# Turning part of the token tiles with VectorE blocks and transfers through DRAM instead of on TensorE, in a delta-rule attention followed by an MLP mixer

## The chip, the cores and the metric

One core of a Trainium2 chip runs the kernel. The metric is the device time of one execution in microseconds (us). Engines are named as the profile names them: PE is TensorE (PEld its weight loads), DVE is VectorE, ACT is ScalarE, POOL is GpSimd and SP is SyncE, whose queue (SPq) issues all transfers of this kernel.

## The reference

Four batch elements, eight heads, 768 tokens, head size 48. A delta-rule recurrence runs over the tokens; its output, seen as 768 tokens x 384 features, goes through a token-mixing and a channel-mixing MLP, each with a residual.

```python
k_n = k / (norm(k) + 1e-6);  state = 0                      # per element and head
for t in range(768):
    y[t]  = q[t] @ state
    state = state + beta[t] * outer(k_n[t], v[t] - k_n[t] @ state)

x  = y as (4, 768, 384)
u  = x + (relu(x.T @ w_tok1) @ w_tok2).T                    # token mixing, 768 -> 256 -> 768
out = u + relu(u @ w_ch1) @ w_ch2                           # channel mixing, 384 -> 1536 -> 384
```

All of it is fp32.

## The kernel before

**Order.** The kernel is a set of generators, one per piece of work, and a string written out by hand says which of them takes its next step. An engine executes its instructions in the order in which they were traced; the waits between engines follow from the data and from the buffers. So the string fixes the order on every engine and on SP's queue. The names in it: `k`, `v` load rows of a pair of chunks, `p` prepares them, `c` and `d` form their products, `t` sends triangular blocks to DRAM (`n_dram`), `i` inverts a round of them on DVE and writes the result (`w_dram`), `f` fetches it (`gm<-w_dram`), `j` joins it, `r` is one step of the recurrence, and `m0` to `m3` are the mixers of the four elements. A mixer begins when its element's recurrence is done, and runs beside the recurrence of the next one. Element 3's mixer runs at the end, beside the last steps of element 2's; what comes after has nothing beside it.

**The mixer.** `mixer(b)` works on `xb`, 128 tokens x 6 tiles x 384 features. First the token phase: `p_1` (L1009), ACT's Relu, and for each of the six tiles c `p_h` (L1022), which DVE adds into `xb[:, c]` (L1026). Then the tokens go in three pairs of tiles (c = 0, 2, 4). For each pair `turn_pair(c)` makes `u_t`, the pair with features on the partitions: for each tile three PE transposes into the PSUM tile `p_ut` (L1032) and one ACT copy (L1036). For elements 1 to 3 (`b >= FAST`) it goes on with `forms(u_t)`, eleven DVE sums of 128x128 blocks (L950), six steps of the generator, some into `t_c` and `t_d`, some in place in `u_t`. `wide_fast` multiplies these forms with sums of the weights in 15 products (L981, PSUM tile `p_r`), which ACT and DVE gather into `r2` (L990, L993, L997). While it ends, DVE makes `s1` and `s2` from `r2` (L1063). Seven products (L1111) in the order a11, a12, s2, s1, a21, a12, a22, twelve (in the middle: six and six) matmuls each, accumulate alternately in `p_o` and `p_o2`, and DVE adds each into `xb` (L1040). Between a11's and the first a12's product stands `turn_pair` of the next pair. `store` writes a finished tile out (L1043).

**Buffers.** `u_t` has one buffer. `t_d`, `s1` and `s2` share the tag `d64` with three buffers, with the staging tiles of the weights early on. The mixer's PSUM tiles (`p_1`, `p_h`, `p_ut`, `p_r`, `p_o`, `p_o2`) share three banks; a tile takes its bank when it is first written.

The order string lets the mixers of elements 2 and 3 overlap so: element 3's six `p_h` steps come while element 2's last pair has done a11, and its `s2` and `s1` products come after them.

Of the kernel before, what the change touches and what calls it, by code (L numbers as in the profile page):

```python
# [8 lines left out]
FP32 = mybir.dt.float32  # L9
# [5 lines left out]
U = 128  # L15
DP = 64
HB = 32
# [6 lines left out]
def kernel(  # L24
# [39 lines left out]
    nc = tc.nc  # L64
# [3 lines left out]
    DM = H * D  # L68
# [15 lines left out]
    loads = ctx.enter_context(tc.tile_pool(name="loads", bufs=2))  # L84
# [6 lines left out]
    dram = ctx.enter_context(  # L91
        tc.tile_pool(name="dram", bufs=2, space=bass.MemoryType.DRAM)
    )
# [7 lines left out]
    def ps_mlp(shape, name):  # L101
        return psum.tile(shape, FP32, name=name, tag="mlp", bufs=3)
# [19 lines left out]
    for i in range(2):  # L122
        r = slice(C * i, C * i + C)
# [25 lines left out]
    for kept, shape in ((kpad, [H, DP]), (qpad, [H, DP]), (kst_of, [NP, 2, D])):  # L149
        for _ in range(NL, NK):  # L150
            n = H * shape[-1]
            flat = lent[:, at : at + n]
# [45 lines left out]
    FAST = 1  # L198
# [7 lines left out]
    for a in cuts[:2]:  # L206
        g = a + NB * GW
# [52 lines left out]
    def piece_of(w, j, col):  # L260
        assert (id(w), j, col - col % WP) in rounded
        return w[:, j]
# [275 lines left out]
    def z_of(u):  # L538
# [9 lines left out]
        out=low16,  # L548
        in_=ident.rearrange("s (q t) -> s q t", t=HB)[:, :, QB:HB],
# [5 lines left out]
        out=even,  # L555
        in_=ident.rearrange("s (q t) -> s q t", t=C)[:, :, 0:HB],
# [4 lines left out]
        out=odd, in0=even, scalar1=-1.0, scalar2=1.0, op0=ALU.mult, op1=ALU.add  # L561
    )
    sides = const.tile([128, 2], FP32, name="sides")
    for i, side in enumerate((even, odd)):
        nc.vector.tensor_tensor(
            out=sides[:, i : i + 1], in0=low16, in1=side, op=ALU.mult
# [435 lines left out]
    def mixer(b):  # L1002

        xb = xbs[b]
        p_1 = [ps_mlp([128, DM], "p_1") for _ in range(NDH)]
        for c in range(NCH):
            assert written.issuperset([NQ * b + 2 * c, NQ * b + 2 * c + 1])
            for dh in range(NDH):
                nc.tensor.matmul(  # L1009
                    p_1[dh], piece_of(w1, c, 0)[:, dh * 128 : (dh + 1) * 128], xb[:, c],  # L1010
                    start=(c == 0), stop=(c == NCH - 1),
                )
            yield
        r1 = []
        for dh in range(NDH):
            r = mlp_pool.tile([128, DM], FP32, name="r1")
            nc.scalar.activation(r, p_1[dh], ACTF.Relu)
            r1.append(r)
        for c in range(NCH):
            p_h = ps_mlp([128, DM], "p_h")  # L1020
            for j in range(NDH):
                nc.tensor.matmul(  # L1022
                    p_h, piece_of(w2, j, c * 128)[:, c * 128 : (c + 1) * 128], r1[j],
                    start=(j == 0), stop=(j == NDH - 1),
                )
            nc.vector.tensor_tensor(out=xb[:, c], in0=xb[:, c], in1=p_h, op=ALU.add)  # L1026
            yield

        def turn(u_t, c):
            p_ut = ps_mlp([128, NCB, 128], "p_ut")  # L1030
            for cb in range(NCB):
                nc.tensor.transpose(  # L1032
                    p_ut[:, cb], xb[:, c, cb * 128 : (cb + 1) * 128], ident
                )
            i = c % 2 * U
            nc.scalar.copy(u_t[:, :, i : i + U], p_ut)  # L1036

        def add(c, half, p):
            e = slice(DH * half, DH * half + DH)
            nc.vector.tensor_tensor(out=xb[:, c, e], in0=xb[:, c, e], in1=p, op=ALU.add)  # L1040

        def store(c, e=slice(0, DM)):
            nc.sync.dma_start(out=out[b, c * 128 : (c + 1) * 128, e], in_=xb[:, c, e])  # L1043

        def turn_pair(c):
            u_t = mlp_pool.tile([128, NCB, 2 * U], FP32, name="u_t", bufs=1)
            for i in range(2):
                turn(u_t, c + i)
                yield
            if b < FAST:  # L1050
                return u_t, None
            f = yield from forms(u_t)
            return u_t, f

        u_t, t_c = yield from turn_pair(0)
        for c in range(0, NCH, 2):

            r2 = mlp_pool.tile([128, NM, 2, 2 * U], FP32, name="r2", bufs=1)
            a11, a12 = r2[:, :, 0, 0:U], r2[:, :, 1, 0:U]
            a21, a22 = r2[:, :, 0, U : 2 * U], r2[:, :, 1, U : 2 * U]  # L1060

            def combine(out, x, y, op, ms):
                nc.vector.tensor_tensor(out=out[:, ms], in0=x[:, ms], in1=y[:, ms], op=op)  # L1063

            made = []

            def halves_of(ms):
                if not made:
                    made.extend(
                        loads.tile([128, NM, U], FP32, name=n, tag="d64", bufs=3)  # L1070
                        for n in ("s1", "s2")
                    )
                s1, s2 = made
                combine(s1, a21, a22, ALU.add, ms)
                combine(s2, s1, a11, ALU.subtract, ms)
                combine(a21, a11, a21, ALU.subtract, ms)

            if b >= FAST:
                for ms in wide_fast(t_c, r2):
                    if ms is not None:  # L1080
                        halves_of(ms)
                    yield
            else:
                for m in range(NM):
                    p_c = ps_mlp([128, 2, 2 * U], "p_c")
                    for k in range(2):
                        f = 2 * m + k
                        for cb in range(NCB):
                            nc.tensor.matmul(  # L1089
                                p_c[:, k],  # L1090
                                piece_of(wc1, cb, f * 128)[:, f * 128 : (f + 1) * 128],
                                u_t[:, cb], start=(cb == 0), stop=(cb == NCB - 1),
                            )
                        if (b, c) == (FAST - 1, NCH - 2):
                            used.add(f)
                        if k == 0:
                            yield
                    nc.scalar.activation(r2[:, m], p_c, ACTF.Relu)
                    yield
                    if m % (NM // 2) == NM // 2 - 1:  # L1100
                        halves_of(slice(m + 1 - NM // 2, m + 1))
                        yield

            s1, s2 = made
            turns = (*range(2, NM), 0, 1) if b >= FAST else range(NM)

            def product(p, a, j, start):
                for i, m in enumerate(turns):
                    block = (2 * m + j // 2,) if j in (0, 2, 3) else (m, "sum", j)
                    assert (id(wc2), *block) in rounded  # L1110
                    nc.tensor.matmul(  # L1111
                        p, a[:, m], wc2[:, m, j],
                        start=(start and i == 0), stop=(i == NM - 1),
                        skip_group_check=True,
                    )
                    if i == NM // 2 - 1:
                        yield


            p_o = ps_mlp([128, DH], "p_o")  # L1120
            p_o2 = ps_mlp([128, DH], "p_o2")
            yield from product(p_o, a11, 0, True)
            add(c, 0, p_o)
            yield
            if c + 2 < NCH:
                u_t, t_c = yield from turn_pair(c + 2)
            yield from product(p_o2, a12, 2, True)
            add(c, 0, p_o2)
            yield
            for ms in (slice(0, NM // 2), slice(NM // 2, NM)):  # L1130
                combine(a12, a12, s2, ALU.subtract, ms)
            yield from product(p_o, s2, 5, False)
            add(c, 1, p_o)
            yield
            yield from product(p_o2, s1, 4, True)
            add(c + 1, 1, p_o2)
            yield
            yield from product(p_o, a21, 1, False)
            add(c + 1, 1, p_o)
            final = (b, c) == (B - 1, NCH - 2)  # L1140
            if final:
                store(c + 1, slice(DH, DM))
            yield
            yield from product(p_o2, a12, 3, False)
            add(c, 1, p_o2)
            store(c)
            yield
            yield from product(p_o, a22, 6, False)
            add(c + 1, 0, p_o)
            store(c + 1, slice(0, DH) if final else slice(0, DM))  # L1150
            yield
# [17 lines left out]
    for b in range(B):  # L1169
        jobs[f"m{b}"] = mixer(b)  # L1170
# [112 lines left out]
    for word in order.split():  # L1283
        name, _, n = word.partition("*")
# [34 lines left out]
```

## Time and profile before

| | us |
|---|---|
| median of the runs | 639.97 (639.02 to 641.68, 3 runs) |
| span of the profiled execution, first to last instruction | 635.6 |
| PE busy in that span | 611.4 |
| DVE busy | 442.5 |
| ACT busy | 261.0 |
| SP queue's transfers, share of 16 DMA engines | 34.7% |

The profiled execution's own device time was not kept beside its span; the median of the runs lies 4.4 us above the span. The mean granted TensorE clock of the span is 0.995. In the profile's lines a group reads: line, engine, operation, output<-input, shapes, count, then busy time and mean ns of one, then the idle time of the engine ahead of it and who ended it. In the chain and the timelines the first two numbers are the start (us from the span's start) and the duration.

### The profile page before, as it was taken

The numbers are of one execution on the slowest core, as the hardware profiler recorded it, in microseconds if no ns is written. First come the engines' busy times: TensorE is split into PE (matmuls) and PEld (weight loads), VectorE is DVE, ScalarE is ACT, GpSimd is POOL, SyncE is SP. The second block draws the span as 40 slices with busy tenths as digits, with TensorE's granted clock in tenths as the row PEclk, the third lists the DMA queues.
The fourth block names the chain that finished last, engine by engine and source line by source line (L and its number), as shares of the span: only waits on it lengthen the run. The fifth ranks groups of instructions, "written<-read, shape, count | busy, mean of one in ns | idle before, by whom it ended". The sixth has DMA issues, their size and how long they took to land.

```text
span 635.6 us, 21584 instructions
## 1 busy us (share of the span) xinstructions
PE 611.4 (96%) x9168; PEld 530.8 (84%) x9168; DVE 442.5 (70%) x1132; ACT 261.0 (41%) x631; POOL 108.2 (17%) x147
## 2 busy tenths in 40 slices
PE   7498899999999999999999999999999999999997
PEld 5457787577888988859899999779999977999997
DVE  4985877997879657987969997785627253373643
ACT  7759887436412243025615333044334130223240
POOL 2438363243210111011110020000000000000000
PEclk9889999999999999999999999999999999999999
DMA  9786667636542454243453213202010000000000
GB/s 172 183 159 149 155 150 188 159 90 146 103 119 64 85 111 110 66 114 74 99 106 87 51 63 69 47 14 36 13 40 3 26 2 1 26 1 25 2 26 26
DMA packets 135776, 50.27 MB, mean 79 GB/s; under 512 B 114656, under 2 KB 130144, under 8 KB 135680
## 3 DMA queue, kind: packets, MB, share of 16 engines
q1 hardware_dynamic: 135680, 48.89, 34.7%
q8 instruction: 72, 1.18, 0.8%
q14 instruction: 24, 0.20, 0.1%
HBM read 39.42 MB, written 9.44 MB: 77 GB/s over the span
## 4 chain that ended last, share of the span: by engine, by line
PE 77%; DVE 4%; ACT 3%; SPq 2%; DMA 1%; issue 1%; DVEq 0%; ACTq 0%
PE p_o L1111 24%; PE p_r L981 19%; PE p_c L1089 6%; PE p_h L1022 5%; PE p L1009 5%; PE p_k L813 3%; PE p_y L833 2%; PE p_s L851 2%; PE p_g L442 2%; PE p_z L773 2%; PE p_y L852 1%; PE p_ut L1032 1%; PE p_w L837 1%; PE p_warm L227 1%; DMA x<-n_dram 1%
## 5 line engine op out<-in xcount | busy, mean ns | idle before, releaser
L1111 PE MATMUL p_o<-wc,r 128*128 128x192 f32 x720 | 127.5, 330 | 0.7 <-ACT u_t L1036 0.6
L1111 PEld LDWEIGHTS p_o<-wc,r 128*128 128x128 f32 x720 | 116.5, 190 | 3.6 <-ACT u_t L1036 1.1
L993 DVE TENSOR_TENSOR r<-r,p_r 128x512 f32<-128x512 f32 x90 | 60.0, 685 | 48.3 <-PE p_r L981 47.7
L990 ACT COPY r<-p_r 128x512 f32<-128x512 f32 x54 | 31.4, 585 | 97.0 <-PE p_r L981 97.0
L1040 DVE TENSOR_TENSOR xb<-xb,p_o 128x192 f32<-128x192 f32 x84 | 29.3, 350 | 53.9 <-PE p_o L1111 53.7
L680 DVE TENSOR_TENSOR x<-x,sub 128x84 f32<-128x84 f32 (+24 forms) x178 | 58.2, 327 | 6.1
L676 DVE TENSOR_TENSOR sub<-x 128x84 f32<-128x84 f32 (+24 forms) x178 | 57.8, 325 | 6.5 <-DMA x<-n_dram 2.5
L1111 PE MATMUL p_o<-wc,s 128*128 128x192 f32 x288 | 50.5, 329 | 0.3 <-DVE xb L1040 0.3
L1089 PE MATMUL p_c<-u_t,wc 128*128 128x256 f32 x216 | 50.2, 384 | 0.1
L1111 PEld LDWEIGHTS p_o<-wc,s 128*128 128x128 f32 x288 | 46.8, 190 | 1.2 <-DVE xb L1040 0.6
L416 POOL TENSOR_TENSOR v_st<-v_st,nrm 128x384 f32<-128x384 f32 x24 | 20.3, 845 | 153.0 <-DMA v_st<-in_v_dram 121.6
L442 PE MATMUL p_g<-kq 48*64 48x128 f32 (+1 forms) x704 | 37.0, 282 | 8.9 <-ACT kq L511 6.6
L997 ACT ACTIVATE r<-r 128x512 f32<-128x512 f32 x54 | 33.9, 631 | 28.2 <-DVE r L993 27.9
L1089 PEld LDWEIGHTS p_c<-u_t,wc 128*128 128x128 f32 x216 | 39.9, 190 | 5.7 <-ACT u_t L1036 0.4
L865 ACT ACTIVATE xb<-p_y 64x192 f32<-64x192 f32 x96 | 31.1, 324 | 29.4 <-DMA out_dram<-xb 13.8
L499 POOL TENSOR_TENSOR mb<-mask_c,cs 128x512 f32<-128x512 f32 x20 | 20.9, 1045 | 129.8 <-DVE gm L445 85.8
L981 PE MATMUL p_r<-u_t,wc 128*128 128x128 f32 x288 | 38.9, 278 | 0.0
L442 PEld LDWEIGHTS p_g<-kq 48*64 48x64 f32 (+1 forms) x704 | 25.9, 136 | 14.6 <-ACT kq L511 9.3
L981 PE MATMUL p_r<-t_d,wc 128*128 128x128 f32 x288 | 37.7, 281 | 0.0
L981 PEld LDWEIGHTS p_r<-u_t,wc 128*128 128x128 f32 x288 | 35.3, 192 | 0.5
L981 PEld LDWEIGHTS p_r<-t_d,wc 128*128 128x128 f32 x288 | 34.1, 191 | 1.0
L843 ACT COPY w_t<-p_w 128x192 f32<-128x192 f32 x48 | 15.2, 316 | 46.2 <-PE p_w L837 45.0
(176 smaller groups left out, 1247.4 us busy)
## 6 DMA issues: line engine op xcount, KB each, us to landing
d<-in_moe_w_ch_dram SPq DMA_DIRECT2D x24, 384.0 KB, 4.5
v_st<-in_v_dram SPq DMA_DIRECT2D x96, 48.0 KB, 2.6
out_dram<-xb SPq DMA_DIRECT2D x23, 192.0 KB, 1.9
kst<-in_k_dram SPq DMA_DIRECT2D x64, 48.0 KB, 3.1
n_dram<-gm SPq DMA_DIRECT2D x72, 32.0 KB, 2.1
pads<-in_k_dram SPq DMA_DIRECT2D x24, 96.0 KB, 3.1
pads<-in_q_dram SPq DMA_DIRECT2D x24, 96.0 KB, 2.6
gm<-w_dram SPq DMA_DIRECT2D x72, 32.0 KB, 2.1
```

Of the source, the lines that this page charges most:

```text
L442: nc.tensor.matmul(p_g[PAR[i ^ cc], p], kqt[f, p, cc, 0], kqt[f, p, cc])
L676: nc.vector.tensor_tensor(out=tmp, in0=col.to_broadcast(dims), in1=row.to_broadcast(dims), op=ALU.mult,)
L680: nc.vector.tensor_tensor(out=new, in0=new, in1=tmp, op=ALU.add)
L865: nc.scalar.mul(y[:, :, D * i : D * i + D], p_y[PAR[1 - i]], 1.0 if c else -1.0)
L981: nc.tensor.matmul(p[:, i], pieces[i // width][:, at : at + 128], f[f"u{n}"], start=first and i == 0, stop=True, skip_group_check=True,)
L990: nc.scalar.copy(o, p)
L993: nc.vector.tensor_tensor(out=o, in0=o, in1=p, op=ALU.add if sign > 0 else ALU.subtract)
L997: nc.scalar.activation(o, o, ACTF.Relu)
L1009: nc.tensor.matmul(p_1[dh], piece_of(w1, c, 0)[:, dh * 128 : (dh + 1) * 128], xb[:, c], start=(c == 0), stop=(c == NCH - 1),)
L1022: nc.tensor.matmul(p_h, piece_of(w2, j, c * 128)[:, c * 128 : (c + 1) * 128], r1[j], start=(j == 0), stop=(j == NDH - 1),)
L1089: nc.tensor.matmul(p_c[:, k], piece_of(wc1, cb, f * 128)[:, f * 128 : (f + 1) * 128], u_t[:, cb], start=(cb == 0), stop=(cb == NCB - 1),)
L1111: nc.tensor.matmul(p, a[:, m], wc2[:, m, j], start=(start and i == 0), stop=(i == NM - 1), skip_group_check=True,)
```

## The change

For elements 1 to 3 and tiles 2 to 5, DVE transposes the tile in blocks of 32x32 as soon as the `p_h` sum is in it, into a staging tile `u_z` (tag `d64`, one for two tiles). Four transfers per tile write the blocks to a DRAM tile of 384 features x 256 tokens, so that a block's row becomes a run of 32 tokens (128 bytes) of one feature's row. `turn_pair` of these two pairs then issues a single transfer from DRAM into `u_t` in place of six PE transposes and two ACT copies. The eleven sums of `forms` no longer stand in `turn_pair` but are taken in steps behind the sums of the s2, s1, a21 and a12 products; `turn_pair` keeps its eight steps, so the order string stays as it is. The first pair of each element, and all of element 0, stay as they were.

```diff
     def mixer(b):
         xb = xbs[b]
+        away = {}
...
             nc.vector.tensor_tensor(out=xb[:, c], in0=xb[:, c], in1=p_h, op=ALU.add)
+            if b >= FAST and c >= 2:
+                if c % 2 == 0:
+                    flat = loads.tile([128, 2, DM], FP32, name="u_z", tag="d64", bufs=3)
+                    away[c] = dram.tile([DM, 2 * U], FP32, name="u_dram")
+                nc.vector.transpose(flat[:, c % 2], xb[:, c])
+                rows = away[c - c % 2].rearrange("(g j) t -> j g t", j=HB)
+                for t in range(U // HB):
+                    r = slice(HB * t, HB * t + HB)
+                    i = c % 2 * U + HB * t
+                    nc.sync.dma_start(
+                        out=rows[:, :, i : i + HB],
+                        in_=flat[r, c % 2].rearrange("p (g n) -> p g n", n=HB),
+                    )
             yield
...
+        coming = []
         def turn_pair(c):
             u_t = mlp_pool.tile([128, NCB, 2 * U], FP32, name="u_t", bufs=1)
+            if c in away:
+                nc.sync.dma_start(
+                    out=u_t, in_=away.pop(c).rearrange("(k f) t -> f k t", f=128)
+                )
+                coming.append(forms(u_t))
+                for _ in range(8):
+                    yield
+                return u_t, None
...
+        def form():
+            if coming:
+                try:
+                    next(coming[0])
+                except StopIteration as end:
+                    coming.clear()
+                    return end.value
...
             yield from product(p_o, s2, 5, False)
             add(c, 1, p_o)
             yield
+            form()
             yield from product(p_o2, s1, 4, True)
             add(c + 1, 1, p_o2)
+            form()
+            form()
             yield
             yield from product(p_o, a21, 1, False)
             add(c + 1, 1, p_o)
+            form()
+            form()
...
             yield from product(p_o2, a12, 3, False)
             add(c, 1, p_o2)
+            form()
+            t_c = form() or t_c
             store(c)
```

## The prediction

> **What bounds the kernel now.** I read the page's busy shares and chain first, then the chain in order of time, the group of the removed instruction, and the timelines of VectorE (DVE) and of SyncE's queue (SPq) in the three stages that change.
>
> ```profile
> span 635.6 us, 21584 instructions
> PE 611.4 (96%) x9168; PEld 530.8 (84%) x9168; DVE 442.5 (70%) x1132; ACT 261.0 (41%) x631; POOL 108.2 (17%) x147
> PE 77%; DVE 4%; ACT 3%; SPq 2%; DMA 1%; issue 1%; DVEq 0%; ACTq 0%
> L1032 PE MATMUL p_ut<-ident,xb x72: 272/273/329, 133.2 to 592.2; 128*128 128x128 f32 x72
> ...
> 319.54 0.81 PE p_ut L1032 x6
> 354.75 0.65 PE p_ut L1032 x6
> 449.65 0.65 PE p_ut L1032 x6
> 486.21 0.81 PE p_ut L1032 x6
> 563.13 0.34 PE p_ut L1032 x3
> 563.55 0.49 ACT u_t L1036
> 564.08 12.08 PE p_o L1111 x72
> 591.78 0.34 PE p_ut L1032 x3
> 592.73 12.07 PE p_o L1111 x72
> ```
>
> The first three lines are the page's: TensorE (PE) is busy 96% of the span and holds 77% of the chain that ended last. The fourth is the group of the transposes. The rest is the chain in order of time. There the second and third pairs of elements 1 to 3 show up, two tiles of three transposes each, and all of them lie on the chain: whatever PE saves there, the kernel saves, unless something else becomes late. The order of work is written out by hand and every engine takes its queue in order, so one late instruction holds all behind it.
>
> **What is removed.** 36 transposes, 12 ACT copies and, in element 3, a wait. Elements 1 and 2 save the four chain pieces: 0.81 + 0.65 + 0.65 + 0.81 = 2.92 us. In element 3 the product that follows a pair starts at 564.08, 0.95 after the transposes at 563.13: p_o2 gets its PSUM bank only when the first copy has emptied p_ut. The other pair is the same (592.73 - 591.78 = 0.95). Without p_ut the bank is free, so 1.90. Sum of the gain: **4.82 us**. ACT's copies save nothing more: it is busy 41% and the chain shows it only in these waits.
>
> The Trainium skill (TensorE: Matmul & The Clock Gate, Part 4) puts a transpose at about 275 ns in a kernel, and the group's 273 ns agrees; by that rule 36 of them are an estimated 9.9 us. But in the chain six take 0.65 to 0.81 us, since the 273 overlap one another, so I take the chain.
>
> **What is added on DVE.** Twelve transposes 128x384, four behind each element's last four p_h adds. No such shape is in the trace; the nearest rows:
>
> ```profile
> L368 DVE STREAM_TRANSPOSE kq<-pads 128x512 f32<-128x512 f32 x24 | 26.6, 1116 | 2.5 <-DMA pads<-in_q_dram 1.8 <-PE p_k L813 0.5
> L749 DVE STREAM_TRANSPOSE t<-gm 128x256 f32<-128x256 f32 x22 | 9.6, 437 | 5.0 <-DMA gm<-w_dram 3.0 <-ACT gm L731 0.9 <-PE p_z L773 0.8
> L693 DVE STREAM_TRANSPOSE r<-x 128x1024 f32<-128x1024 f32 x2 | 2.5, 1234 | 0.0
> ```
>
> 256 columns take 437 ns and 1024 take 1234, a line that gives 0.57 us for 384. The bounds are 0.44 and 0.84 (384/512 of L368, whose elements are scattered). Ours read and write whole rows, as the two rows of the line nearly do: 0.57, and about 0.5 of pace, since neighbours on DVE overlap by 0.08.
>
> In element 2 this meets a full DVE, which is inverting blocks beside it:
>
> ```profile
> 424.90 0.54 DVE L1026 TENSOR_TENSOR xb<-xb,p_h 128x384 f32<-128x384 f32 x1
> 425.69 0.55 DVE L1026 TENSOR_TENSOR xb<-xb,p_h 128x384 f32<-128x384 f32 x1 [0.25 <-PE p_h L1022]
> 426.31 0.36 DVE L820 TENSOR_TENSOR rest<-p_k,v_st 128x192 f32<-128x192 f32 x1
> 427.08 0.18 PE p_y L833
> ```
>
> Four transposes come ahead of `rest`, whose reader p_w stands among the p_y at 427.08. 4 x 0.5 = 2.0, less the 0.25 idle and the 0.4 from rest's end (426.67) to 427.08: PE stands **1.3 us** there (0.5 to 2.5 with the bounds). In element 1 DVE has idle time enough between the p_h adds; I cost it at nothing beside the next term, which takes in 0.4 of it if that cover fails. forms() of the second and third pair is the same eleven instructions, moved behind the s2, s1, a21 and a12 products; DVE waits for PE there (DVE 70% busy), so nothing, and up to 1 us in element 1, where blocks are inverted beside it.
>
> **What is added on SP's queue.** Sixteen writes per element (32 partitions x 12 pieces of 128 B), each waiting for its DVE transpose, and two reads of u_t. SP takes them in order, so whatever is queued behind waits too. The price of an issue:
>
> ```profile
> L612 SPq DMA_DIRECT2D n_dram<-gm x72: 303/449/1912, 73.7 to 392.5; - x72
> L403 SPq DMA_DIRECT2D kst<-in_k_dram x64: 595/614/1745, 14.8 to 352.7; - x64
> DMA to landing us min/median/max: 2.2/3.1/7.1
> n_dram<-gm SPq DMA_DIRECT2D x72, 32.0 KB, 2.1
> d<-in_moe_w_ch_dram SPq DMA_DIRECT2D x24, 384.0 KB, 4.5
> SPq L696 <- DVE x L682: 18.2, 1, 18.2
> ```
>
> A write of 256 pieces of 128 B holds SP 0.45 us (0.30 at best, landing 2.1); 384 pieces by proportion 0.67. I take 0.5, near the row of the same kind, with 0.30 and 0.67 as the ends. (The landing line is L403's, the last one a wait of SP in element 2.) In element 1 the queue has no room:
>
> ```profile
> 281.38 0.35 SPq L696 DMA_DIRECT2D w_dram<-x  x1
> 282.81 1.77 SPq L359 DMA_DIRECT2D pads<-in_q_dram  x4
> 284.62 7.53 SPq L637 DMA_DIRECT2D gm<-w_dram  x10
> 292.24 1.35 SPq L359 DMA_DIRECT2D pads<-in_k_dram  x3
> 294.68 4.01 SPq L403 DMA_DIRECT2D kst<-in_k_dram  x4
> 300.96 0.53 ACT L465 ACTIVATE ksq<-kst 128x384 f32<-128x384 f32 x1
> 302.57 0.34 DVE L860 TENSOR_TENSOR s_t<-s_t,p_s 128x192 f32<-128x192 f32 x1
> 303.79 0.62 PE p_k L813 x16
> 314.96 0.53 ACT L465 ACTIVATE ksq<-kst 128x384 f32<-128x384 f32 x1 [0.48 <-DMA kst<-in_k_dram]
> ```
>
> From 282.81 to 298.69 SP issues almost without a gap, 15.9 us of work. The new writes start when the third p_h add and its transpose are done, about 282.3, and all sixteen stand ahead of the ten gm reads and the kst loads. With 16 x 0.5 = 8 us of them kst's last issue ends at 282.3 + 8.0 + 15.9 = 306.2 instead of 298.69: 7.5 late, or 2.9 if the long issues (7.53 for ten gm, 4.01 for four kst, 4.6 more than at 0.45 and 0.61 each) shrink because what they stood for is over by then. kst landed at most 0.7 before ksq reads it (298.69 + 2.2 against 300.96 leaves about none). ksq feeds a reduction on DVE directly ahead of s_t, which ends 0.88 before PE's p_k at 303.79. Slack 1.5 together: PE stands 1.4 to 6.0 there. I take **4.0 us**, a little above the middle, since nothing shows what the long issues stand for (the ends of the issue price, 3 less or more, make it 0 to 8.7). It isn't won back soon: the next kst load is already waited for at 314.96. In element 2 SP has nothing to do while the writes go out (one wait of 18.2 us, for the end of the inversion) and the loads behind them move by 3 us, with work ahead of their readers: nothing, 2 us if that cover goes.
>
> The Trainium skill (Perfetto Trace Analysis, What "DMA-bound" means) calls a sequencer's track of solid DMA slices a bound of its own, in which only larger descriptors help. The stretch above is such a track; by that rule alone the change, which queues 6144 pieces of 128 B per element, is a loss.
>
> The u_t reads carry 384 KB (nearest row 4.5 us to landing) and are asked for one product ahead of a12 and s2, 2 x 12 matmuls or 3.9 us before the first form(); DVE might wait 0.6, and has about 1.4 idle per product (the row of 537.14 below): nothing.
>
> **What is added as a wait in element 3.** The writes' staging tile shares three buffers with t_d, s1 and s2. When element 3's second staging tile (c = 4) is wanted, s1 and s2 of element 2's last pair are in use, so it gets the first one's buffer, and the transpose of c = 4 waits until the eight writes of c = 2 and 3 have landed. Behind it on DVE stand these:
>
> ```profile
> 531.32 0.56 DVE L1026 TENSOR_TENSOR xb<-xb,p_h 128x384 f32<-128x384 f32 x1 [0.74 <-PE p_h L1022]
> 533.90 0.55 DVE L1026 TENSOR_TENSOR xb<-xb,p_h 128x384 f32<-128x384 f32 x1 [0.74 <-PE p_h L1022]
> 537.14 0.35 DVE L1040 TENSOR_TENSOR xb<-xb,p_o 128x192 f32<-128x192 f32 x1 [1.40 <-PE p_o L1111]
> 536.94 4.06 PE L1111 MATMUL p_o<-wc,s 128*128 128x192 f32 x24
> ```
>
> The add of c = 2 starts at 531.32, its transpose ends at 532.4, eight issues follow until 536.4, the last lands 2.1 after its start, at 538.0. Then transpose 0.57, add 0.56, transpose 0.57, with overlaps 539.5, and the add of 537.14 ends at 539.85. The s1 product, the second half of the 24 matmuls, starts into that p_o2 at 538.9: PE stands **1.0 us** (0 at 0.30 per issue, 2.4 at 0.67). The other transposes of element 3 fit between the adds (0.74 idle each).
>
> **The sum.** -4.8 + 4.0 + 1.3 + 1.0 = +1.5 us on a span of 635.6. The runs shown have a median of 639.97, 4.4 above that span; I carry that over: 641.5 us.
>
> **Rivals.** (a) *The waits are hidden.* If an issue costs 0.30 and the long issues shrink, SP's sixteen take 4.8, kst is no later than now (282.3 + 4.8 + 11.3 = 298.4), and the wait in element 3 is gone: -4.8 plus 0.5 to 1.3 in element 2 gives 635.7 to 636.5. For it: DVE's idle time, and the 0.30 in L612's row; against it, that row's median. It ends faster. (b) *SP's queue becomes the bound of element 1.* At 0.67 per issue the sixteen take 10.7, PE stands 6.7 there, 2.4 in element 3, 1.3 in element 2: -4.8 + 10.4 = +5.6, 645.6 us, and 647.6 if the long issues all stay. It decides from about 0.57 per issue (16 issues in element 1 and eight in element 3 for each 0.07 us), where the sum passes 3.2. For it: kst's 0.61; against: those are loads. (c) *A transpose costs PE its full duration.* 36 x 0.273 = 9.8 instead of 4.8 makes -3.5, 636.5 us. Only the rule cited above speaks for it; the chain speaks against.
>
> **How the numbers follow.** About 0.5% (3.2 us) is what a measurement of this kernel can tell from no change: 636.8 to 643.2. Forecast, costs that eat the gain: 0.43. (a) 0.19, (c) 0.03, together faster 0.22. (b), with element 1 anywhere above 5.7, 0.35. Predicted is the forecast's 641.5. Its own range is 638.5 to 643.2; that for 8 in 10 takes in most of (a) and (b): 635.8 to 647.
>
> **What would show it.** Right: no p_ut in the second and third pairs; element 1's ksq waiting for kst several us around 300, and PE's gap behind it; SPq rows of the new writes near 0.5; in element 3 the transpose of c = 4 waiting for a DMA, 4 us after its add, and PE waiting for the add of 537. Wrong: writes at 0.3 or 0.7 per issue; kst's loads in time although SP is late; a u_t read that holds DVE at the first form(); the transposes at 1 us.

## The result and the profile after

| | before | after |
|---|---|---|
| median of 6 runs each, us | 640.81 (636.54 to 647.2) | 650.04 (648.0 to 653.99) |
| ratio after/before, 95% interval | | 1.0154 (1.0124 to 1.0184) |
| profiled execution: span, time, us | 635.6, - | 649.5, 651.27 |

The kernel became 9.2 us slower by the medians. Without the slowest execution of before (647.2, 1.7% above the fastest) they lie 10.1 us apart. The forecast was 641.5, in a range of 635.8 to 647.

The page of the changed kernel, in the same three lines as shown of before:

```profile
span 649.5 us, 21589 instructions
PE 615.0 (95%) x9132; PEld 531.8 (82%) x9132; DVE 448.6 (69%) x1144; ACT 255.7 (39%) x619; POOL 108.1 (17%) x147
PE 72%; DVE 10%; ACT 9%; DMA 3%; SPq 3%; issue 2%; DVEq 0%; ACTq 0%
```

PE's share of the chain fell from 77% to 72%, and DVE's rose from 4% to 10%. To find where the time went I compared when the same instruction starts in both traces:

| instruction | before, us | after, us | lag |
|---|---|---|---|
| third `p_h` add of element 1 | 281.24 | 285.67 | 4.4 |
| last `p_h` add of element 1 | 285.51 | 290.50 | 5.0 |
| second `p_r` add of element 1 | 296.94 | 309.68 | 12.7 |
| a `p_r` add of element 1's third pair | 378.66 | 392.53 | 13.9 |
| third `p_h` add of element 2 | 421.09 | 434.74 | 13.6 |
| second `p_r` add of element 2 | 434.06 | 449.24 | 15.2 |
| third `p_h` add of element 3 | 531.32 | 545.61 | 14.3 |
| the add of element 3's s1 | 541.04 | 556.34 | 15.3 |
| last `xb` add | 632.70 | 646.41 | 13.7 |

So 13.7 us arise in the profiled execution. The third `p_h` add of an element is the last instruction ahead of its first new one, so 4.4 of them stand there before the change can act. The change itself (differences of the unrounded times): +0.6 up to the last `p_h` add of element 1, among which DVE's new transposes stand, +7.8 from there to the second `p_r` add, +0.9 in the rest of element 1, +1.5 and -0.9 in element 2, +1.0 and -1.6 in element 3; together 9.3, close to the medians' 9.2.

The place of the 7.8 is told by five views. First SP's queue (start, duration, line, transfer):

```profile
285.81 0.35 SPq L696 DMA_DIRECT2D w_dram<-x  x1
286.83 2.17 SPq L1037 DMA_DIRECT2D u_dram<-u_z  x4
289.09 1.37 SPq L359 DMA_DIRECT2D pads<-in_q_dram  x3
290.56 3.02 SPq L1037 DMA_DIRECT2D u_dram<-u_z  x4
293.62 0.48 SPq L359 DMA_DIRECT2D pads<-in_q_dram  x1
294.20 5.49 SPq L1037 DMA_DIRECT2D u_dram<-u_z  x8
299.74 4.94 SPq L637 DMA_DIRECT2D gm<-w_dram  x10
...
307.21 3.72 SPq L403 DMA_DIRECT2D kst<-in_k_dram  x4
```

Sixteen writes hold SP for 2.17 + 3.02 + 5.49 = 10.7 us. The `gm` reads behind them start at 299.74; before they started at 284.62. That is 15.1 us later, 10.1 more than the 5.0 of lag already there. Then the reader of that `gm`, a DVE transpose, before:

```profile
291.00 0.42 DVE L749 STREAM_TRANSPOSE t<-gm 128x256 f32<-128x256 f32 x1
293.31 0.68 DVE L993 TENSOR_TENSOR r<-r,p_r 128x512 f32<-128x512 f32 x1
```

and after, with the wait in brackets (the last two lines are element 3's):

```profile
302.80 0.45 DVE L749 STREAM_TRANSPOSE t<-gm 128x256 f32<-128x256 f32 x1 [6.67 <-DMA gm<-w_dram]
...
303.54 0.35 DVE L820 TENSOR_TENSOR rest<-p_k,v_st 128x192 f32<-128x192 f32 x1
...
305.14 0.68 DVE L993 TENSOR_TENSOR r<-r,p_r 128x512 f32<-128x512 f32 x1
...
552.16 0.58 DVE L1032 STREAM_TRANSPOSE u_z<-xb 128x384 f32<-128x384 f32 x1 [3.42 <-DMA u_dram<-u_z]
553.72 0.32 DVE L1054 TENSOR_TENSOR xb<-xb,p_o 128x192 f32<-128x192 f32 x1
```

Before, the transpose of `gm` had no wait at all; now DVE stands 6.67 us. Behind it on DVE is `rest`, which PE's `p_w` needs. PE's longest wait between 280 and 335 (us in total, times, longest):

```profile
PE p_w L837 <- DVE rest L820: 5.5, 2, 5.2
```

The lag is 7.8 and PE stands only 5.2 there. The rest shows in the stretches of time (stretch, length, busy time of PE, PEld, DVE, ACT, POOL, then the granted TensorE clock):

```profile
238.00:242.00 4.00, 2.66 (x45) 2.16 (x37) 2.87 (x9) 1.68 (x5) 0.00 (x0) 0.88 0.57 133
242.00:246.00 4.00, 4.00 (x42) 3.05 (x42) 1.18 (x3) 0.68 (x2) 1.20 (x2) 0.69 0.41 85
...
298.00:302.00 4.00, 0.84 (x8) 0.60 (x6) 0.00 (x0) 0.33 (x1) 0.00 (x0) 1.00 0.55 83
302.00:306.00 4.00, 1.96 (x53) 1.99 (x54) 3.16 (x10) 0.76 (x2) 0.00 (x0) 0.56 0.44 68
306.00:310.00 4.00, 4.00 (x92) 3.79 (x94) 2.55 (x5) 1.43 (x5) 1.87 (x2) 0.59 0.52 109
310.00:314.00 4.00, 4.00 (x138) 3.83 (x132) 2.25 (x5) 2.93 (x8) 0.00 (x0) 1.00 0.44 86
```

Behind the standing, PE works at a clock of 0.56 and 0.59: 1.96 x 0.44 + 4.00 x 0.41 = 2.5 us more for the same work. 5.2 + 2.5 = 7.7, nearly all of the lag. In the kernel before no stretch of 4 us from 200 us on is below 0.97. The first two lines are ahead of the change and explain part of the 4.4: 1.34 us of standing, then 0.3 + 1.2 us by the clock.

In element 1's third pair the moved `forms` (L950) meet a DVE that inverts blocks. One of them on DVE's timeline:

```profile
380.84 0.35 DVE L1054 TENSOR_TENSOR xb<-xb,p_o 128x192 f32<-128x192 f32 x1
381.10 0.28 DVE L950 TENSOR_TENSOR u_t<-u_t 128x128 f32<-128x128 f32 x1
381.31 0.38 DVE L676 TENSOR_TENSOR sub<-x 128x220 f32<-128x220 f32 x1
```

Before, all eleven of this pair stood together and were done by 359.6; now the last ones share DVE with L676 and L680, and `xb` adds come late behind them. The price of the new instructions, in groups and in the DMA issues:

```profile
L1032 DVE STREAM_TRANSPOSE u_z<-xb x12: 578/578/580, 286.2 to 553.2; 128x384 f32<-128x384 f32 x12
L1037 SPq DMA_DIRECT2D u_dram<-u_z x48: 302/476/1966, 286.8 to 556.2; - x48
L1064 SPq DMA_DIRECT2D u_t<-u_dram x6: 377/382/1393, 335.6 to 604.4; - x6
DMA to landing us min/median/max: 1.7/2.8/3.9
```

The transposes cost the 0.57 forecast. An issue costs 0.476 at the median, as forecast (0.5), but up to 1.97. The landing line is L1037's, from an issue to the arrival of its data.

### The profile page after: what moved, and what is told of

Its sections match the earlier page's. It is cut to its first block, busy times and chain, and to the rows that moved or that the text cites. A ratio compares the mean times of both kernels' runs of the same rounds, so it can differ in the third digit from the quotient of the medians.

```text
span 649.5 us, 21589 instructions
## 1 busy us (share of the span) xinstructions
PE 615.0 (95%) x9132; PEld 531.8 (82%) x9132; DVE 448.6 (69%) x1144; ACT 255.7 (39%) x619; POOL 108.1 (17%) x147
## 4 chain that ended last, share of the span: by engine, by line
PE 72%; DVE 10%; ACT 9%; DMA 3%; SPq 3%; issue 2%; DVEq 0%; ACTq 0%
PE p_o L1143 23%; PE p_r L981 18%; PE p_c L1121 7%; PE p L1010 4%; PE p_g L442 3%; PE p_s L851 2%; PE p_h L1023 2%; PE p_k L813 2%; PE p_z L773 2%; PE p_warm L227 2%; PE p_y L833 2%; DVE x L680 1%; DVE sub L676 1%; PE p_w L837 1%; DVE kq L368 1%
## 5 line engine op out<-in xcount | busy, mean ns | idle before, releaser
L680 DVE TENSOR_TENSOR x<-x,sub 128x84 f32<-128x84 f32 (+24 forms) x178 | 59.8, 336 | 6.1
L676 DVE TENSOR_TENSOR sub<-x 128x84 f32<-128x84 f32 (+24 forms) x178 | 57.1, 321 | 5.8 <-DMA x<-n_dram 1.8
L1121 PE MATMUL p_c<-u_t,wc 128*128 128x256 f32 x216 | 51.9, 394 | 0.1
L843 ACT COPY w_t<-p_w 128x192 f32<-128x192 f32 x48 | 15.2, 317 | 60.1 <-PE p_w L837 58.8
```

The costliest lines, as they stand in the source:

```text
L676: nc.vector.tensor_tensor(out=tmp, in0=col.to_broadcast(dims), in1=row.to_broadcast(dims), op=ALU.mult,)
L680: nc.vector.tensor_tensor(out=new, in0=new, in1=tmp, op=ALU.add)
L1121: nc.tensor.matmul(p_c[:, k], piece_of(wc1, cb, f * 128)[:, f * 128 : (f + 1) * 128], u_t[:, cb], start=(cb == 0), stop=(cb == NCB - 1),)
```

## The experiments

Theory at the start: the sixteen writes on SP's queue hold back element 1's `gm` reads and cost nearly all; DVE's transposes and the late `forms` cost the rest. Rivals: DVE's added work; element 2's and 3's waits; and, later, whether the low clock behind a standing PE is a price of its own. Ratios are to the kernel before.

**e1: the change in element 1 alone.**

```diff
-            if b >= FAST and c >= 2:
+            if b == 1 and c >= 2:
```

> The change is made in element 1 alone; elements 2 and 3 turn their tiles on TensorE as before. Theory (SP's queue): almost the whole loss sits here. In the changed kernel's profile VectorE waited 6.67 us for gm<-w_dram behind the sixteen writes, the late forms() held PE about 2.4 us at the start of the third pair, and 1.46 us are saved: +7 to +10 us against before, ratio 1.011 to 1.016. Rival (VectorE's transposes cost where they stand, a third of them in each element): +2 to +4 us, ratio 1.003 to 1.006.

Measured 649.02, ratio 1.0129 (1.0073 to 1.0184). The lag is 1.9 at the third `p_h` add, 2.5 ahead of the `gm` read, 10.8 behind it and 11.8 at the end of element 1, and it stays there. Element 1 alone is the loss.

**e2: the change in elements 2 and 3 alone.**

```diff
-            if b >= FAST and c >= 2:
+            if b >= 2 and c >= 2:
```

> The change is made in elements 2 and 3 alone. Theory (SP's queue of element 1): losses 1.3 us (rest behind the transposes, element 2) and 1.3 us (staging buffer, element 3) against a gain of 1.46 + 1.90: -0.8 us, ratio 0.997 to 1.001. Rival (the transposes and writes cost the same in each element): +5 to +7 us, ratio 1.008 to 1.011.

Measured 643.77, ratio 1.005 (1.0016 to 1.0084): a miss. Element 2 cost 1.5 and won back 0.9, a net loss of 0.6 us where a gain of 0.2 was expected. In element 3 the lag grew by 4.5 before 1.6 came back. Its staging wait (DVE's timeline), and PE's wait for the add behind it, and the stretches of time:

```profile
541.95 0.58 DVE L1032 STREAM_TRANSPOSE u_z<-xb 128x384 f32<-128x384 f32 x1 [5.26 <-DMA u_dram<-u_z]
```

```profile
PE p_o L1143 <- DVE xb L1054: 2.6, 1, 2.6
```

```profile
541.00:545.00 4.00, 1.41 (x9) 1.13 (x8) 3.02 (x7) 0.00 (x0) 0.00 (x0) 1.00 0.26 38
545.00:549.00 4.00, 4.00 (x17) 3.91 (x16) 0.37 (x2) 0.48 (x1) 0.00 (x0) 0.58 0.41 60
```

The transpose waited 5.26 us, not 3.42, so PE stood 2.6 instead of 0.7, and then the clock fell to 0.58 for 4 us: 1.7 more. In the changed kernel 0.7 us of standing there brought no lower clock. Why the wait was longer stays open (SP held the sixteen issues 11.7 us here against 10.4).

**e3: the writes from ACT's queue.**

```diff
-                    nc.sync.dma_start(
+                    nc.scalar.dma_start(
```

> The changed kernel with the 48 writes issued from ScalarE's queue instead of SP's; all else is the same, the same bytes in the same pieces. Theory (the order of SP's queue): VectorE's wait of 6.67 us for gm<-w_dram in element 1 goes, the kernel is 5 to 7 us faster than the changed one, +2 to +4 against before, if ScalarE's own 8 us of issues per element stay beside its work. Rival 1 (the transfers themselves, 128 B pieces on the DMA engines, make the loads late): nothing changes, +9. Rival 2 (VectorE's transposes): nothing changes, +9.

Measured 665.93, ratio 1.0382 (1.0335 to 1.043): the largest miss, 16 us slower than the changed kernel. SP was relieved as meant: DVE's wait for `gm` was gone. But ACT's own work now stood behind the writes (its waits, then the first of them on its timeline; ACTq is its queue):

```profile
ACT w_t L843 <- DMA u_dram<-u_z: 8.0, 1, 8.0
ACT gm L754 <- DMA u_dram<-u_z: 5.7, 1, 5.7
ACT ksq L465 <- DMA u_dram<-u_z: 4.3, 1, 4.3
```

```profile
284.94 2.18 ACTq L1037 DMA_DIRECT2D u_dram<-u_z  x4
287.17 0.32 ACT L843 COPY w_t<-p_w 128x192 f32<-128x192 f32 x1 [7.99 <-DMA u_dram<-u_z]
```

Of the 8.0 us ACT spent 2.2 issuing four writes; before that it waited for the tile that they write, whose transpose starts at 284.33. In the waits of 5.7 and 4.3 the issues take 4.0 and 3.3. `w_t` lies on the recurrence's chain. The Trainium skill (DMA: Bandwidth & Descriptors, Issuing engines are not separate DMA queues) says that starting transfers on several engines only saves the sequencer's time for starting them, which it calls usually small beside the transfer. One issue is small here too, 0.476 us against a landing of 2.8 at the median, but sixteen in a row hold SP for 10.7 us, and on ACT they hold up an engine that computes; the measurement decides.

**e4: DVE's transposes alone**, added to the kernel before, nobody reads them.

```diff
+            if b >= FAST and c >= 2:
+                if c % 2 == 0:
+                    flat = loads.tile([128, 2, DM], FP32, name="u_z", tag="d64", bufs=3)
+                nc.vector.transpose(flat[:, c % 2], xb[:, c])
```

> The kernel before with the twelve VectorE transposes added into a staging tile that nobody reads: no writes, no u_t from DRAM, TensorE turns all tiles, forms() at its old place. Theory: 0.4 us in element 1, 1.3 us in element 2, nothing in element 3, +1.7 us, ratio 1.001 to 1.005. Rival (VectorE's time is the loss): +7 to +10 us, ratio above 1.010.

Measured 641.88, ratio 1.0006 (0.9981 to 1.003). In the trace they cost 0.6 to 1.0 us in element 1 (0.6 of it among the `p_h` adds), 1.5 in element 2 and nothing in element 3; the time can't tell that from none.

**e5: `forms` taken late alone**, turns on PE as before.

```diff
+            if c >= 2:
+                coming.append(forms(u_t))
+                for _ in range(6):
+                    yield
+                return u_t, None
             f = yield from forms(u_t)
```

> The kernel before with one edit: TensorE turns all tiles as before, but the eleven sums of forms() of the second and third pairs are taken behind the s2, s1, a21 and a12 products, as in the changed kernel. No transposes on VectorE, no transfers. Theory: in element 1 VectorE is full while the second pair's products run, so the third pair's first forms product waits 2 to 2.5 us for the late sums; elsewhere nothing: +2 to +2.5 us, ratio 1.002 to 1.006. Rival (the late sums fill idle time of VectorE everywhere, the 2.4 us of the changed kernel's profile came from its backlog of transposes): 0, ratio 0.998 to 1.002.

Measured 641.98, ratio 1.0022 (0.9996 to 1.0048); in the trace the lag is 1.5 us larger in element 1's third pair and 1.2 at the element's end, and nothing is lost elsewhere.

**e6: the sixteen writes alone**, in element 1 of the kernel before, straight from `xb` and read by nobody.

```diff
+            if b == 1 and c >= 2:
+                rows = ...
+                for t in range(U // HB):
+                    nc.sync.dma_start(out=rows[:, :, HB * t : HB * t + HB],
+                        in_=xb[HB * t : HB * t + HB, c].rearrange("p (g n) -> p g n", n=HB))
```

> The kernel before plus sixteen writes in element 1 alone, of the same shape (32 partitions x 12 pieces of 128 B) and at the same place of SP's queue as in the changed kernel, straight from xb into a DRAM tile that nobody reads. No transposes, no late forms(), nothing saved. Theory (SP's queue): 16 x 0.48 to 0.65 us ahead of gm<-w_dram, VectorE waits 6 to 7 us for it, +6 to +8 us, ratio 1.009 to 1.013. Rival (it takes the transposes too, or the loss is elsewhere): below +3 us.

Measured 648.73, ratio 1.0123 (1.0091 to 1.0155). Dead transfers cost as much as element 1's whole change. The lag rises from 0.1 to 9.2 in the same place and stays. DVE's wait, and the stretches of time:

```profile
DVE t L749 <- DMA gm<-w_dram: 6.5, 1, 6.5
```

```profile
294.00:298.00 4.00, 0.00 (x0) 0.00 (x0) 0.21 (x1) 0.00 (x0) 0.00 (x0) 0.89 0.49 76
298.00:302.00 4.00, 2.98 (x83) 3.01 (x85) 3.53 (x11) 0.97 (x3) 0.52 (x1) 0.50 0.51 90
302.00:306.00 4.00, 4.00 (x92) 3.68 (x91) 2.34 (x4) 1.21 (x4) 1.36 (x2) 0.50 0.41 83
```

PE stood 5.1 us and then ran at 0.50.

**e7: the same bytes in four writes** of 128 rows of 1536 bytes, dead as well.

```diff
+            if b == 1 and c >= 2:
+                nc.sync.dma_start(out=dram.tile([U, DM], FP32, name="u_dram"), in_=xb[:, c])
```

> As the run with sixteen dead writes in element 1, but each tile goes out in one write of 128 rows of 1536 B, four issues in place of sixteen, the same bytes. Theory (the number of issues on SP's queue): 4 x 0.36 us, +0 to +2 us, ratio 1.000 to 1.003. Rival (the bytes and their landing in DRAM, or the wait for the p_h sums at that place of the queue): as much as sixteen, +6 to +8 us.

Measured 643.42, ratio 1.0021 (0.9991 to 1.0051). SP's rows and DVE's wait:

```profile
287.08 0.38 SPq L1028 DMA_DIRECT2D u_dram<-xb  x1
290.49 0.88 SPq L1028 DMA_DIRECT2D u_dram<-xb  x2
```

```profile
DVE t L749 <- DMA gm<-w_dram: 1.6, 2, 1.1
```

A wide write holds SP 0.37 to 0.40 us, no longer than a narrow one, and moves four times as much. It is SP's time ahead of the `gm` reads that counts, and not the traffic: 1.6 us for the four issues against 9.2 for the sixteen of e6. Most of this is their number; but a wide write also has 128 pieces in place of 384, so the number of pieces isn't separated from it here.

**e8: element 3 alone, with the second staging tile in a buffer that is free there.**

```diff
-            if b >= FAST and c >= 2:
+            if b == 3 and c >= 2:
...
+                    if c == 4:
+                        flat = pads[:, :, 0, 0:DM]
...
```

> The change in element 3 alone, and its second staging tile lies in the load buffer of q and k, which is free by then, so the transpose of c = 4 has nothing to wait for. Theory (the wait for the staging buffer costs element 3 what it cost in the changed kernel, 1.3 us, and 4 us in the run with elements 2 and 3): no wait of VectorE for u_dram, and the whole 1.6 to 1.9 us are gained, ratio 0.996 to 0.999. Rival (the writes themselves hold something else in element 3): no gain, ratio 1.000 to 1.004.

Measured 639.14, ratio 0.9944 (0.9906 to 0.9982): faster than the kernel before. No transpose waits for a transfer, and the lag falls by 0.8 per pair, 1.6 in all. The time fell by more than the trace shows (2.1 us by the medians).

**e9: all elements, one write per tile, and the shuffle in the reads** (four per pair).

```diff
...
-                for t in range(U // HB):
-                    ...
+                nc.sync.dma_start(out=away[c - c % 2][i : i + U], in_=flat[:, c % 2])
...
-                nc.sync.dma_start(out=u_t, in_=...)
+                rows = away.pop(c).rearrange("(t j) (k g n) -> g j k t n", j=HB, n=HB, g=U // HB)
+                for g in range(U // HB):
+                    nc.sync.dma_start(out=u_t[HB * g : HB * g + HB].rearrange("j k (t n) -> j k t n", n=HB), in_=rows[g])
```

> The changed kernel with the gathering moved from the writes to the reads: each turned tile goes to DRAM in one write of 128 rows of 1536 B (4 issues per element in place of 16), and u_t comes back in four reads of 32 partitions x 24 pieces of 128 B, asked for between two products (8 per element in place of 2). All else, the late forms() too, is the same. Theory (the issues in front of gm<-w_dram in element 1): the wait of 6.7 us falls to 1 to 2, the kernel is 5 to 8 us faster than the changed one, +1 to +4 us against before, ratio 1.001 to 1.006. Rival 1 (the small pieces cost wherever they are): as slow as the changed one, ratio 1.012 to 1.018. Rival 2 (the reads land too late for forms()): VectorE waits for u_dram at the first sums of each pair, ratio above 1.006.

Measured 643.9, ratio 1.006 (1.0031 to 1.0088): 6 us of the loss are gone, with four issues in place of sixteen ahead of the `gm` reads. What is left sits mostly in element 1 and in part moved to the reads, as rival 2 had it (DVE's waits in element 1):

```profile
DVE t L749 <- DMA gm<-w_dram: 1.2, 1, 1.2
```

```profile
DVE t_d L950 <- DMA u_t<-u_dram: 3.0, 1, 3.0
```

Across this second wait, and one of 1.7 us for a `gm` right behind it, the lag rises from 1.8 to 6.0 us; it is 5.3 at the end, against 0.8 ahead of the first new instruction.

The Trainium skill (Perfetto Trace Analysis, What "DMA-bound" means) says that where a sequencer's track is solid, larger descriptors are what matters. e7 and e9 agree: with 1536-byte pieces in place of 128, the loss of e6 goes from 1.0123 to 1.0021 and that of the change from 1.0154 to 1.006.

**e10: elements 2 and 3 only, transposes and writes later**, between the products of the first pair, where DVE and SP have room.

```diff
-        ... wide_fast(...)
+        for n, ms in enumerate(wide_fast(...)):
+            if b >= 2 and c == 0 and n in (3, 8, 13, 18):
+                send(2 + (n - 3) // 5)
...
```

`send(c)` holds the transpose of tile c and its four writes.

> The change in elements 2 and 3 alone, and the transposes and their sixteen writes stand behind the 4th, 9th, 14th and 19th step of the first pair's forms products instead of behind the p_h sums: there VectorE is about half idle, SP has little to do, and s1 and s2 of the element before are out of use. Theory: the 1.2 us of element 2 (rest behind the transposes) and the wait of element 3 for its staging buffer go, what is saved stays (1.2 + 1.6 to 1.9 us): -2.8 to -3.3 us against before, ratio 0.994 to 0.997. Rival (a later read of u_t or the transposes between the sums of p_r cost as much): 0.998 to 1.003.

Measured 638.92, ratio 0.9966 (0.994 to 0.9993): beats both kernels, by 2.3 us by the medians and 1.5 in the trace where 2.8 to 3.3 were expected. Element 3 keeps its gain (lag -1.6). Element 2 loses 1.0 and gains 0.9: a `gm` read is late behind the new writes (SP's queue, then its reader on DVE).

```profile
435.01 3.97 SPq L1041 DMA_DIRECT2D u_dram<-u_z  x8
439.02 1.88 SPq L637 DMA_DIRECT2D gm<-w_dram  x2
```

```profile
445.08 0.45 DVE L749 STREAM_TRANSPOSE t<-gm 128x256 f32<-128x256 f32 x1 [1.60 <-DMA gm<-w_dram]
```

**e11 and e12: ten dead products in PE's wait**, in e6 and in the changed kernel, to see what the clock is worth.

```diff
+        if t == 27:
+            for _ in range(10):
+                nc.tensor.matmul(p_warm, ident, wc1[:, 0, 0:512].rearrange("p (a b) -> p a b", b=128))
         p_y = ps_seq([128, NP, D], "p_y")
```

> The kernel before with the sixteen dead writes in element 1 (as in e6) and ten dead PE products of 128x128x512 into the spare warm-up bank, put ahead of the p_y and p_w products at which PE stood. In e6 PE stood there 5.1 us (stretches 290 to 302) and then ran 4.2 us short of its work at a granted clock of 0.50 to 0.83 (stretches 298 to 310: 2.98 x 0.50 + 4.00 x 0.50 + 4.00 x 0.17). At full clock the ten products fill 10 x 0.45 = 4.5 us of the wait (0.45 from 24 products of 192 columns in 4.06 us). Theory, the lower clock follows PE's standing idle: no stretch near 300 is below 1.00, the wait of DVE for gm stays at 6.5 us, and the loss of e6 against the kernel before (8 to 9 us) shrinks by 3.5 to 4.5 us, to about 5, ratio 1.007 to 1.008. Rival, the lower clock comes from something else (the traffic, the kind of work behind the wait): the clock stays near 0.5 there and the loss stays at 8 to 9 us, ratio 1.012.

> The changed kernel with the same ten dead PE products at the same place of element 1. There PE stood 5.2 us and then lost 2.5 us at a granted clock of 0.56 to 0.59 (302 to 310). Theory, the clock follows the standing: DVE's wait for gm stays at 6 to 7 us, the clock near 300 is 1.00, and the time is about 2.5 us below the changed kernel's 650, 647.5; ratio to the kernel before 1.010 to 1.012. Rival, the clock is lowered by something else: no better than the changed kernel, ratio 1.015.

Measured 650.49, ratio 1.0151 (1.01 to 1.0203), and 650.45, ratio 1.0178 (1.0135 to 1.0221): no gain. The filling was mis-sized. On PE's timeline of e12 each product is two instructions:

```profile
294.09 8.75 PE L830 MATMUL p_warm<-wc,ident 128*128 128x512 f32 x20
```

8.75 us instead of 4.5, 3.5 longer than the wait. The clock of e12 did stay at 1.00 in all stretches from 286 to 314, so the fall at this place follows PE's standing; what it is worth was covered by the overshoot.

**e13 and e14: five such products.**

```diff
-            for _ in range(10):
+            for _ in range(5):
```

> The kernel before with the sixteen dead writes in element 1 (as in e6) and five dead PE products of 128x128x512 ahead of the p_y and p_w at which PE stood for 5.1 us. Ten took 8.75 us, so five take 4.4 and end inside the wait. Theory, the low clock behind the wait is the price of PE's standing: the clock near 300 is 1.00, the loss in element 1 falls from 9.1 to about 5 us, ratio near 1.008. Rival, the clock behind the wait is worth nothing, because other engines or loads bound PE there anyway: the clock is 1.00 too, and the loss stays at 8 to 9 us, ratio 1.012 to 1.014.

> The changed kernel with the same five dead PE products (4.4 us) in the wait of 5.2 us of element 1. Theory: clock 1.00 behind the wait, the lag of element 1's first p_r additions falls from 7.7 us to about 5.2, and the time is 2.5 us below the changed kernel's, ratio to the kernel before 1.010 to 1.012. Rival: the lag stays at 7.7 and the ratio at 1.015.

Measured 648.44, ratio 1.011 (1.0078 to 1.0141), and 649.38, ratio 1.0116 (1.0088 to 1.0145). The stretches of e13 that answer to those of e6:

```profile
294.00:298.00 4.00, 4.00 (x18) 2.33 (x18) 0.00 (x0) 0.59 (x1) 0.00 (x0) 1.00 0.54 81
298.00:302.00 4.00, 3.20 (x82) 2.11 (x81) 2.75 (x9) 0.78 (x2) 0.00 (x0) 1.00 0.43 66
302.00:306.00 4.00, 4.00 (x132) 3.78 (x125) 2.96 (x6) 2.40 (x8) 1.83 (x2) 1.00 0.55 116
```

DVE still waits 6.6 us for `gm` in e13 and 6.0 in e14; only the clock differs. From the fifth `p_h` add to the `w_t` copy behind the slow stretch the lag grows by 6.3 in e13 against 9.1 in e6, and by 5.1 in e14 against 7.7 in the changed kernel: 2.8 and 2.6 us less, without any work taken away. For e14 the time agrees with the theory (1.010 to 1.012 expected), for e13 it fell less than expected (1.008), and the intervals of both overlap those of the kernels without filling. Nor does the gain of e14 last in its profiled execution. From the third `p_h` add of element 1 to the end its lag grows by 9.6 us, no less than the 9.3 of the changed kernel: it loses 2.2 in the rest of element 1 (0.8 in the changed kernel) and 3.1 at the start of element 2 (1.5). There PE stood 0.93 us, as it does in the changed kernel, but only in e14 did the clock fall behind it:

```profile
436.00:440.00 4.00, 3.51 (x66) 3.20 (x69) 3.14 (x16) 0.91 (x2) 0.00 (x0) 0.60 0.44 65
```

So the price of the clock is shown in the traces of the stretch itself, 2.5 to 2.8 us. That filling the wait makes the whole kernel faster is not shown, and what makes the clock fall behind a short standing in one execution and not in another stays open.

## Why the prediction was wrong

- **Gain, -4.82.** The mechanism held, the size in part: element 3 won back 1.6 of 1.90 and element 2 0.9 of 1.46. What element 1 won is covered by the losses there. Why element 2 won so little stays open.
- **SP's queue in element 1, +4.0: the step that failed.** That the writes would hold up what is queued behind them on SP was right, but the path and the size were not. (1) The reader was another: the prediction followed the queue to the `kst` loads and measured the slack of `ksq`, though it had the ten `gm` reads in the same fence, ahead of `kst`. Their reader at 291.00 has DVE's queue behind it, and it waited 6.67 us. `ksq` itself, the sign that was named, starts at 313.82 without a wait. (2) The issue price: 0.476 at the median is the 0.5 taken, but the sixteen took 10.7 us, the upper end 0.67, because single issues take up to 1.97. (The ten `gm` issues did shrink, 7.53 to 4.94, as the lower bound allowed.) With both, PE stood 5.2 us; that this lies inside the range given is luck, since the range was worked out for `ksq`. (3) Not priced at all: the clock behind the standing, 2.5 us by the stretches and 2.6 by the slow stretch of e14. Measured 7.8, and 8.3 with the 0.6 of DVE's transposes, against 4.0 for both.
- **DVE in element 1 and `forms` late, at nothing.** Wrong by about 2.4 us: the rest of element 1 lost 0.9 where 1.46 should have been won. e5 finds 1.2 of it and e4 up to 0.4; the rest stays open. The prediction named up to 1 us for `forms` and 0.4 for the transposes if their covers fail; both failed. DVE's 70% is a mean of the span; in the changed kernel DVE is busy 3.8 us of every 4 from 376 to 392.
- **Element 2, +1.3.** Measured 1.5, in e4 too.
- **Element 3, +1.0.** Measured 1.0, through the staging buffer as told: the transpose of c = 4 starts 4.0 us after its add. In e2 it was 4.5, where PE stood long enough for the clock to fall. e8 takes the wait away and wins.
- **The sum.** The forecast was +1.5, the trace shows +9.3. Of the 7.8 between them 4.3 lie in element 1's token phase, 2.4 in the rest of element 1 and 1.1 in elements 2 and 3.
- **The 4.4 added to the span** were not all outside it: the changed kernel's execution has 1.8 there (651.27 - 649.5). By this figure the execution of before took about 637.4, an estimate; the rest was its distance to the median, and doesn't touch the difference forecast.
- **Rivals.** (b), SP's queue as the bound of element 1, is what happened, with its 0.67 per issue, though through `gm` and not `kst`; its time of 645.6 falls short mainly by the clock and the rest of element 1. (a) and (c) are refuted: the waits weren't hidden, and the transposes taken from PE gave back no more than the chain had shown.

## What to carry to other kernels

When transfers are put on a queue that is taken in order, list everything queued behind them and find the earliest reader with no slack, and count issues, not bytes: by the trace sixteen narrow ones cost 9 us, four wide ones with the same bytes about 1. Then add to a forecast stall of TensorE what a lower clock behind it can cost, here 2.5 us behind 5.2. A change that helps in one stage and hurts in another can be applied by stage: element 3 alone (0.9944 of the time before), or elements 2 and 3 with later writes (0.9966), is faster than before.

## What the runs showed of the hardware

- A standing PE can pay twice. After 5.1 to 5.2 us of standing the granted clock was 0.50 to 0.59 in two stretches of 4 us, after 2.6 us it was 0.58 in one stretch, after 1.34 us 0.69, and after 0.7 us 1.00; after 0.93 us it was 0.60 in e14 and 1.00 in the changed kernel. The Trainium skill (TensorE: Matmul & The Clock Gate, Part 1: The HAM clock gate) gives half rate after an idle window of about 3.4 us and full rate again after as much work. The 0.50 agrees; 1.34 and 0.93 us are much shorter than that window, so its figure is no safe limit here.
- An issue's time doesn't grow with its bytes: 0.476 us at the median for 48 KB in 384 pieces, 0.37 to 0.40 for 192 KB in 128 (e7). More pieces may cost more: the reads of e9, 96 KB in 768 pieces, took 0.65 at the median.
- A transfer queued on ACT holds ACT's computing while it waits for its data and while it is issued: 8.0, 5.7 and 4.3 us in e3.
